# Joined additions, GpSimd Newton steps and a re-ordered start in an attention and MoE kernel

## The chip, the cores and the metric

The kernel runs on one core of one Trainium2 chip. The metric is the device time of one execution in microseconds (us). Five engines matter: TensorE (PE; PEld is its weight load), VectorE (DVE), ScalarE (ACT), GpSimd (POOL) and SyncE (SP), which here issues the DMAs. Each runs its own queue strictly in order and waits on semaphores for the others.

## The reference, cut to what matters

The inputs q, k and v have 2 batches, 8 heads, 768 positions and 64 dimensions. Each head has 16 centroids; every query and key is assigned to the centroid with the largest cosine similarity, and attention is allowed only inside a cluster.

```
q_n, k_n, c_n = each / (norm + 1e-06)
q_assign = argmax(q_n . c_n);  k_assign = argmax(k_n . c_n)
mask   = q_assign[..., :, None] == k_assign[..., None, :]
scores = where(mask, q @ k.T / 8, -1e9)
attn   = exp(scores - max);  attn /= sum(attn) + 1e-9
x = attn @ v                                     # 1536 x 512 after a reshape
h = x @ w_in;  x = (max(h,0) + alpha*min(h,0)) @ w_out
xn = x / rms(x) * rms_g;  x = (silu(xn @ w_gate) * (xn @ w_val)) @ w_out2
```

## The kernel before, in words

**Tiling.** The 16 head-batches are worked off as 8 pairs. A pair has two phases (one half of its 384 query columns each), a phase six slots, one for each tile of 128 keys: slot `6 * ph + t`. In a slot TensorE makes the scores of the tile for both heads (L712 and L713 into one of three rotating `ps_st` banks), ScalarE takes their exponential (`p`, L714), and TensorE multiplies earlier `p` tiles with v (L728). The row maximum of each query has to be known before its exponential, so TensorE also makes the masked scores once ahead (`max_tile`, L662), VectorE reduces them (`mx`, L664; L666 in the first phase), splits the maximum into two parts (`mh`, L671, L672), and TensorE turns them (L690) into rows of the operand `op`.

**What is prepared.** For each pair ahead of its phases: loads (`raw` and `nat`, the transposed and the plain form of q and k), squares (`sq`, ACT L469), sums of squares (`ss`, DVE L483), the reciprocal root (`norm`, `rnorm`), scores against the centroids (`sims`, L516 to L543), the cluster's one-hot code (`arg`: L552 to L565), its transpose (`oht`), and the operand's high part and residual (`hi` L606, `lo` L614, which go to `op` by a DMA). `rnorm` takes two integer operations (L435, L437), three Newton steps and three last operations (L440 to L442). A Newton step is three VectorE operations (L429 to L431), or four GpSimd ones (L423 to L426) for the pairs in `NEWTON`.

**Sums of the softmax.** `pv_tiles` sums `p` over the keys with matmuls against ones (L739, into `ps_sm`). In the phases of `SUMMED` (4 to 12), the first four `p` tiles are added in pairs on VectorE (`pair_add`, L747), so that four operands are left, two sums and two `p`. In the phases of `WHOLE`, here 10 and 11, `pair_join` (L751) adds the two sums in place, and three operands are left.

**Start.** Pairs 0 and 1 have a start of their own (`start`, from L336): squares from `raw`, column sums by a matmul (`ss_rows`, L494), a copy, a turn (`ss_turn`, L503), and `root` (n_y L399, n_e L400, and n_s L403, which copies the sums out of PSUM so that the bank can be used again). `oht_direct(h)` turns the one-hot code of head h of pair 0 by 30 small matmuls for both heads (L589): head 0 into the two-bank tiles `ps_pv` and `ps_mx`, head 1 into `ps_pr` and the three `ps_st` banks; ScalarE copies them to rows 64 to 80 of `op_0` and `op_1` (L598, L600). The first `max_tile` reads `op_0`.

**What sets the order.** Nothing is scheduled at run time. `plan()` puts every step into a slot with an order number inside the slot. The tables `FIRST` to `FIFTH` (pairs 0 to 4) and `PAIR` (pairs 5 to 7) give for each step (slot, order) relative to the pair's first slot, 12 times the pair's number; a negative slot lies in earlier pairs' phases. Steps with one slot are issued by order number, and each engine's queue follows from that. The two MoE layers (L1010 and on) come after the attention.

Of the kernel before, what the change touches and what calls it, by code (L numbers as in the profile page):

```python
# [12 lines left out]
AF = mybir.ActivationFunctionType  # L13
ALU = mybir.AluOpType
# [4 lines left out]
BIG = float(2.0 ** 60)  # L19
# [3 lines left out]
    "load": ((-44, 6.1), (-44, 6.2), (-39, 6.1), (-38, 6.1)),  # L23
    "sq": ((-38, 4), (-36, 1.015)),
    "ss": ((-37, 0.6), (-36, 2.05)),
    "norm": tuple((t, 5 + n / 100) for n, t in enumerate([-32] + [-31] * 6 + [-30] * 7)),
    "hi": ((-28, 1.06), (-27, 1.06)),
    "lo": ((-24, 2.3), (-25, 1.05)),
    "sims": ((-30, 1.6), (-29, 1.7)),
    "scale": ((-29, 1.75),),  # L30
    "arg": ((-27, 5), (-24, 2.1), (-24, 2.2), (-22, 1.62), (-21, 5)),
# [3 lines left out]
FIFTH = {  # L35
    **PAIR,
    "lo": ((-26, 2.3), (-25, 1.05)),
    "load": ((-41, 6.1), (-41, 6.2), (-39, 6.1), (-38, 6.1)),
    "sq": ((-35, 4), (-34, 4)),
    "ss": ((-34, 5), (-33, 5)),  # L40
}
FOURTH = {
    **PAIR,
    "load": ((-38, 6.1), (-38, 6.2), (-30, 6.1), (-30, 6.2)),
    "sq": ((-32, 4), (-32, 4.1)),
    "ss": ((-30, 2.2), (-30, 2.3)),
    "norm": tuple((-27 + n // 6, 5 + (n % 6) / 10) for n in range(17)),
    "hi": ((-27, 4), (-26, 4)),
# [9 lines left out]
    "sq": ((-24, 4), (-23, 4)),  # L58
    "ss": ((-24, 5), (-23, 5)),
    "norm": tuple((-21, 5.1 + n / 100) for n in range(14)) + tuple((-18, 2.41 + n / 100) for n in range(3)),  # L60
    "hi": ((-22, 4), (-21, 4)),
    "lo": ((-18, 2.46), (-14, 6)),
    "sims": ((-20, 1.65), (-18, 1.7)),
    "scale": ((-18, 2.44),),
    "arg": ((-18, 2.45), (-16, 5), (-16, 5.1), (-15, 5), (-14, 5)),
# [23 lines left out]

SUMMED = range(4, 13)  # L90
FULL = (4, 6, 8, 10)
WHOLE = {10: (6, 1.99), 11: (5, 0.59)}
SQUARED = 2
ASIDE = (2,)
NEWTON = (2, 3)
EARLY = (
    (59, 12),
    (70, 2.45),
# [127 lines left out]
class Attention:  # L226
# [52 lines left out]
    def setup(self):  # L279

        nc, C, H, D = self.nc, self.C, self.H, self.D
        v, act, g = nc.vector, nc.scalar, nc.gpsimd
        n, rows = H * C, 2 * C
        cn = self.pre([n, 2, D], "cn")
        css = self.pre([n, 1], "css")
        self.sq0 = self.pre([128, D], "sq0")
        src = self.centroids.rearrange("h c d -> (h c) d")
# [29 lines left out]
        i = self.idf.rearrange("p (e g r) -> p g e r", e=2, r=32)  # L317
# [27 lines left out]
        self.warm(6, self.bk.pv)
        rc = self.bk.st()
        for i in range(0, 128, rows):
            nc.tensor.matmul(rc[i:i + rows, 0:1], lhsT=self.idf[:rows, :rows], rhs=r[:rows], start=True, stop=True)
        act.copy(out=self.rc0, in_=rc[:, 0:1])
        ps = self.bk.pr()  # L350
        self.sims_mm(0, ps)
        self.prep_sq(1, 0)
        simc = self.sims_copy(0, ps, self.rc0)
        ssc = self.ss_rows(0, v.tensor_copy)
        for h in range(2):
            self.prep_dma_a(h)
        for h in range(2):
            self.prep_dma_b(h, 1)
        self.load_v(0)
        steps, rn = self.root(self.ss_turn(ssc), [128, self.T // 2, 4, 2], "n0")  # L360
        self.sims_turn(0, self.bk.st(), simc)
        spread(self.cb, n, act.copy)
        self.prep_sq(1, 1)
        for step in steps:
            step()
        self.norm[0] = None, rn
# [5 lines left out]
        self.sims_mm(1, ps)  # L372
        ssc = self.ss_rows(1, act.copy)
        self.simc[1] = self.sims_copy(1, ps, 1.0)
        self.norm[1] = self.root(self.ss_turn(ssc), [128, self.T // 2, 4, 2], "n1", True)
        act.add_instruction(mybir.InstLoadActFuncSet(name=nc.get_next_instruction_name(), act_func_set_id=EXP_AND_LN,
                                                     ins=[], outs=[]))
        act.activation(out=spare, in_=self.eps[:, 0:1], func=AF.Exp)
        self.warm(4, self.bk.pv)
        self.prep_lo(0, 1)  # L380
        for h in range(2):
            self.oht_direct(h)
        for i in range(2):
            self.prep_hi(1, i)
        v.tensor_tensor_reduce(out=pat, in0=pat, in1=self.idf, scale=1.0, scalar=0.0, op0=ALU.mult, op1=ALU.add,
# [191 lines left out]
    def oht_direct(self, h):  # L577

        nc, X = self.nc, self.T // 2
        if h:  # L580
            hi = [self.bk.pr(), self.bk.st()]
            ps = [[self.bk.st(), self.bk.st()], hi]
        else:
            ps = [b().rearrange("p a b -> p (a b)") for b in (self.bk.mx, self.bk.pv)]
            ps = [[b, b[:, self.HS:]] for b in ps]
        for i in (1, 0):
            for g in range(2):
                for x in range(X):
                    nc.tensor.matmul(ps[i][g][0:16, x * 128:(x + 1) * 128], lhsT=self.oh[0][:, x, h, :, i, g],  # L589
                                     rhs=self.idr, start=True, stop=True)  # L590
        o1 = self.op1[h][64:80]
        for i in (1, 0):
            cuts = ((0, 128), (128, self.S)) if not i else ((0, self.S),)
            parts = [(ps[i][g][:16, :self.HS], o1[:, i, sl]) for g, sl in self.halves()] if h else \
                [(ps[i][0][:16, a:b], o1[:, i, a:b]) for a, b in cuts]
            for src, dst in parts:
                if i:
                    nc.scalar.copy(out=dst, in_=src)  # L598
                else:
                    nc.scalar.activation(out=dst, in_=src, func=AF.Identity, scale=-BIG)  # L600

# [198 lines left out]
    def plan(self):  # L800
# [3 lines left out]
        def at(s, o, fn, *a):  # L804
            ev.setdefault(s, []).append((o, len(ev.get(s, [])), fn, a))
# [4 lines left out]
        for pr in range(self.NP):  # L810
# [564 lines left out]
```

## Time and profile before

| | |
|---|---|
| median of 3 runs | 819.69 us (819.63 to 819.71) |
| profiled execution, device time | 819.63 us |
| its span | 817.9 us |
| PE busy | 809.6 us, 99% |
| DVE busy | 623.7 us, 76% |
| ACT busy | 335.6 us, 41% |
| POOL busy | 362.1 us, 44% |
| granted TensorE clock | 1.00 |

The span is what the profile's times run over; the profiled execution's own time is 1.7 us longer and lies 0.06 us under the median. A busy share of an engine is an average over very different stretches: the first 60 us fill the pipeline, 60 to about 275 us are attention phases, and the rest is matrix multiplication for the MoE layers.

### The profile page before, as it was taken

To read this page: it belongs to the slowest core of one execution; us is meant where nothing else is said; L and a number is where in the kernel's file an instruction comes from. 1 tells how busy PE (TensorE), PEld (TensorE's weight loads), DVE (VectorE), ACT (ScalarE), POOL (GpSimd) and SP (SyncE) were. 2 spreads that over 40 slices of the span, in tenths; PEclk is the share of its full clock that TensorE was granted. 3 is DMA by queue.
4 is the path that set the end of the run, shared out by engine and by line. 5 is a ranking of instruction groups with operands and counts; after the bars stand their busy time and mean duration, and the time that the engine had idled before them with its cause. 6 is when DMAs were issued, how large, how long until landed. Compare 5 with 4: busy or idle time off the path is not lost.

```text
span 817.9 us, 11705 instructions
## 1 busy us (share of the span) xinstructions
PE 809.6 (99%) x4350; PEld 625.0 (76%) x4350; DVE 623.7 (76%) x1036; ACT 335.6 (41%) x652; POOL 362.1 (44%) x335
## 2 busy tenths in 40 slices
PE   8999999999999999999999999999999999999998
PEld 5565666666666888888888888888888888888887
DVE  6989999999998489999999977877555555555523
ACT  7655776666564333433434444432212221222110
POOL 3421221221213267786766772416465546554511
PEclk9999999999999999999999999999999999999999
DMA  8786655754532022232212220102121212121012
GB/s 206 201 229 181 132 154 161 171 111 115 133 114 79 1 77 78 78 103 65 88 59 75 77 78 1 51 1 78 52 77 54 76 52 77 57 73 51 1 52 103
DMA packets 23624, 74.03 MB, mean 91 GB/s; under 512 B 3600, under 2 KB 4752, under 8 KB 23568
## 3 DMA queue, kind: packets, MB, share of 16 engines
q1 hardware_dynamic: 23568, 73.29, 31.3%
q8 instruction: 34, 0.56, 0.3%
q14 instruction: 22, 0.18, 0.1%
HBM read 49.88 MB, written 3.15 MB: 65 GB/s over the span
## 4 chain that ended last, share of the span: by engine, by line
PE 96%; DVE 2%; DMA 1%; ACT 1%; issue 0%; SPq 0%; DVEq 0%; ACTq 0%
PE ps_st L1010 35%; PE ps_mx L1010 14%; PE ps_pv L1010 14%; PE ps_pv L728 8%; PE ps_pr L1010 5%; PE ps_st L712 4%; PE ps_st L713 4%; PE ps_sm L739 3%; PE ps_ma L662 3%; PE ps_mb L662 2%; DMA nat<-in_kn_dram 1%; DVE mx L666 1%; PE ps_pv L393 1%; PE ps_pr L516 1%; PE ps_pr L690 0%; PE ps_pr L782 0%
## 5 line engine op out<-in xcount | busy, mean ns | idle before, releaser
L1077 POOL TENSOR_TENSOR gl<-v,gh 128x512 fp32r<-128x512 f32 x68 | 96.0, 1412 | 143.8 <-ACT gh L1076 142.4
L1076 ACT CAST gh<-v 128x512 fp32r<-128x512 f32 x68 | 42.3, 622 | 151.9 <-DVE v L1073 83.3
L1073 DVE TENSOR_TENSOR v<-ps_st,t 128x512 f32<-128x512 f32 x36 | 24.9, 691 | 100.3 <-PE ps_st L1010 100.2
L714 ACT ACTIVATE p<-ps_st 128x384 f32<-128x384 f32 x192 | 85.3, 491 | 28.1 <-PE ps_st L713 26.6
L992 DVE SCALAR_TENSOR_TENSOR dec_a<-raw,dec_a 128x512 uint32<-128x512 uint32 x66 | 81.6, 1236 | 2.2
L728 PE MATMUL ps_pv<-p,vnat 128*64 128x384 f32 x384 | 72.6, 499 | 0.0
L1069 DVE SCALAR_TENSOR_TENSOR v<-v,alpha,t 128x512 f32<-128x512 f32 x45 | 53.0, 1177 | 21.9 <-ACT v L1068 21.8
L712 PE MATMUL ps_st<-op 128*128 128x384 f32 x192 | 67.8, 353 | 0.3 <-ACT oht L575 0.3
L1010 PE MATMUL ps_st<-x1h,stage 128*128 128x512 f32 x272 | 67.2, 389 | 0.0
L713 PE MATMUL ps_st<-op 82*128 82x384 f32 x192 | 65.0, 339 | 0.0
L1010 PEld LDWEIGHTS ps_st<-x1h,stage 128*128 128x128 f32 x272 | 51.1, 188 | 10.6
L1123 DVE TENSOR_TENSOR x<-ps_mx,x 128x1024 f32<-128x1024 f32 x36 | 43.9, 1220 | 18.7 <-PE ps_mx L1010 18.7
L664 DVE TENSOR_REDUCE mx<-ps_ma 128x1 f32<-128x384 f32 x90 | 49.7, 552 | 10.1 <-PE ps_ma L662 9.2
L798 POOL TENSOR_TENSOR x1l<-X,x1h 128x384 fp32r<-128x384 f32 x15 | 15.9, 1062 | 91.7 <-ACT x1h L795 91.7
L1010 PE MATMUL ps_st<-x1h,wvh 128*128 128x512 f32 x144 | 56.2, 390 | 0.0
L1010 PE MATMUL ps_st<-x1h,wvl 128*128 128x512 f32 x144 | 56.0, 389 | 0.0
L1010 PE MATMUL ps_st<-x1h,wih 128*128 128x512 f32 x132 | 51.6, 391 | 0.0
L1010 PE MATMUL ps_st<-x1h,wil 128*128 128x512 f32 x132 | 51.4, 389 | 0.0
L664 DVE TENSOR_REDUCE mx<-ps_mb 128x1 f32<-128x384 f32 x90 | 49.4, 549 | 0.1
L1123 DVE TENSOR_TENSOR x<-ps_pv,x 128x1024 f32<-128x1024 f32 x35 | 42.5, 1214 | 6.8 <-PE ps_pv L1010 6.8
L990 DVE TENSOR_SCALAR dec_a<-raw 128x512 uint32<-128x512 uint32 x66 | 47.6, 722 | 0.0
L995 DVE SCALAR_TENSOR_TENSOR dec_e<-raw,dec_e 128x512 f32<-128x512 uint32 x66 | 45.7, 692 | 2.3
(304 smaller groups left out, 1998.3 us busy)
## 6 DMA issues: line engine op xcount, KB each, us to landing
raw<-in_moe_w_out_dram SPq DMA_DIRECT2D x28, 512.0 KB, 3.5
op<-stage SPq DMA_DIRECT2D x32, 384.0 KB, 5.9
raw<-in_moe_w_in_dram SPq DMA_DIRECT2D x15, 512.0 KB, 3.6
raw<-in_moe_w_val_dram SPq DMA_DIRECT2D x12, 512.0 KB, 3.4
raw<-in_moe_w_gate_dram SPq DMA_DIRECT2D x12, 512.0 KB, 3.4
op<-stage SPq DMA_DIRECT2D x16, 288.0 KB, 5.9
raw<-in_qt_dram SPq DMA_DIRECT2D x8, 384.0 KB, 4.8
raw<-in_kt_dram SPq DMA_DIRECT2D x8, 384.0 KB, 5.1
```

Source lines behind the costliest of these rows:

```text
L664: nc.vector.tensor_reduce(out=mx[:, g, k:k + 1], in_=to, op=ALU.max, axis=AX.X)
L712: nc.tensor.matmul(ps, lhsT=o1[:, 1, ks], rhs=o1[:, 0, qs], start=True, stop=False)
L713: nc.tensor.matmul(ps, lhsT=o2[:, 1, ks], rhs=o2[:, 0, qs], start=False, stop=True)
L714: nc.scalar.activation(out=self.P[s][:, e], in_=ps, func=AF.Exp, scale=self.scale)
L728: nc.tensor.matmul(ps[64 * e:64 * e + 64], lhsT=self.vnat[ph // 2][:, e, t0 + y], rhs=P[y][:, e], start=t0 + y == 0, stop=t0 + y == T - 1)
L990: lambda: v.tensor_scalar(out=a, in0=top, scalar1=3, scalar2=0x3FFFFFFF, op0=ALU.logical_shift_left, op1=ALU.bitwise_and),
L992: lambda: v.scalar_tensor_tensor(out=a, in0=top, scalar=0xC0000000, in1=a, op0=ALU.bitwise_and, op1=ALU.bitwise_or),
L995: lambda: v.scalar_tensor_tensor(out=ef, in0=bot, scalar=2.0 ** -52, in1=ef, op0=ALU.mult, op1=ALU.mult),
L1010: self.nc.tensor.matmul(ps, lhsT=a, rhs=b, start=first and i == 0, stop=last and i == len(terms) - 1)
L1069: nc.vector.scalar_tensor_tensor(out=v, in0=v, scalar=self.nalpha[:, a], in1=t, op0=ALU.mult, op1=ALU.add)
L1077: nc.gpsimd.tensor_tensor(out=lo, in0=v, in1=f(hi), op=ALU.subtract)
L1123: nc.vector.tensor_tensor(out=dst, in0=ps, in1=dst, op=ALU.add)
```

## The change

Four things are edited.

1. `WHOLE` gets the phases 4 to 9 as well: `pair_join` at the phase's slot 5 order 5 (even phases) or slot 6 order 1.99 (odd phases), so that TensorE sums three operands there instead of four.
2. `NEWTON` gets pairs 5, 6 and 7: their Newton steps go to GpSimd. The table `PAIR` starts the two integer operations earlier (`norm`).
3. The residual of q (`lo`) is moved: for pairs 5 to 7 from slot -24 to slot -19, for pair 2 from -18 to -12. Loads of pair 4, squares of pair 3 and one high part of pair 2 move by some slots.
4. The start is re-ordered. The square of pair 0's k is split between ScalarE and VectorE, the centroids are scaled on ScalarE, both residuals of pair 0 come early, the sums' rows come ahead of the centroids' scores, and both squares of pair 1 follow the copies of the centroids' block. `oht_direct` comes ahead of `root` of pair 1 and of the loading of the activation table, and its copies for head 0 are divided between ScalarE and VectorE.

```
-    "norm": tuple((t, 5 + n / 100) for n, t in enumerate([-32] + [-31] * 6 + [-30] * 7)),
+    "norm": tuple((t, 5 + n / 100) for n, t in enumerate([-34] * 2 + [-33] * 6 + [-32] * 6 + [-30] * 3)),
-    "lo": ((-24, 2.3), (-25, 1.05)),
+    "lo": ((-19, 4.9), (-25, 1.05)),
...
-    "lo": ((-18, 2.46), (-14, 6)),
+    "lo": ((-12, 2.02), (-14, 6)),
...
-WHOLE = {10: (6, 1.99), 11: (5, 0.59)}
+WHOLE = {**{ph: ((5, 5), (6, 1.99))[ph % 2] for ph in range(4, 10)}, 10: (6, 1.99), 11: (5, 0.59)}
-NEWTON = (2, 3)
+NEWTON = (2, 3, 5, 6, 7)
...
+        self.prep_sq(0, 0)
+        self.prep_hi(0, 0)
+        sq, raw = self.nat[0][:, 1].rearrange("p t h d -> p (t h d)"), self.raw[0][:, 1]
+        (_, s0), (_, s1) = self.halves()
+        act.activation(out=sq[:, s0], in_=raw[:, s0], func=AF.Square)
+        v.tensor_tensor(out=sq[:, s1], in0=raw[:, s1], in1=raw[:, s1], op=ALU.mult)
+        self.prep_hi(0, 1)
         for i in range(2):
-            self.prep_sq(0, i)
-        self.prep_hi(0, 0)
-        self.prep_lo(0, 0)
+            act.activation(out=cn[:, i, :], in_=cn[:, i, :], func=AF.Identity, scale=r)
         for i in range(2):
-            v.tensor_scalar(out=cn[:, i, :], in0=cn[:, i, :], scalar1=r, scalar2=None, op0=ALU.mult)
-        self.prep_hi(0, 1)
+            self.prep_lo(0, i)
         self.warm(6, self.bk.pv)
+        ssc = self.ss_rows(0, act.copy)
...
-        self.prep_sq(1, 0)
-        simc = self.sims_copy(0, ps, self.rc0)
-        ssc = self.ss_rows(0, v.tensor_copy)
...
-        self.sims_turn(0, self.bk.st(), simc)
+        self.sims_turn(0, self.bk.st(), self.sims_copy(0, ps, self.rc0))
         spread(self.cb, n, act.copy)
-        self.prep_sq(1, 1)
+        for i in range(2):
+            self.prep_sq(1, i)
...
-        self.norm[1] = self.root(self.ss_turn(ssc), [128, self.T // 2, 4, 2], "n1", True)
+        ss = self.ss_turn(ssc)
+        self.warm(4, self.bk.pv)
+        self.oht_direct(0)
+        self.norm[1] = self.root(ss, [128, self.T // 2, 4, 2], "n1", True)
+        self.oht_direct(1)
         act.add_instruction(mybir.InstLoadActFuncSet(...))
         act.activation(out=spare, in_=self.eps[:, 0:1], func=AF.Exp)
-        self.warm(4, self.bk.pv)
-        self.prep_lo(0, 1)
-        for h in range(2):
-            self.oht_direct(h)
...
+        cuts = (0, 128), (128, self.S)
         for i in (1, 0):
-            cuts = ((0, 128), (128, self.S)) if not i else ((0, self.S),)
-            parts = [(ps[i][g][:16, :self.HS], o1[:, i, sl]) for g, sl in self.halves()] if h else \
+            parts = [(ps[i][g][:16, :self.HS], o1[:, i, sl]) for g, sl in self.halves()] if h or i else \
                 [(ps[i][0][:16, a:b], o1[:, i, a:b]) for a, b in cuts]
-            for src, dst in parts:
+            for n, (src, dst) in enumerate(parts):
+                aside = n == (1 if i else 0) and (i or not h)
                 if i:
-                    nc.scalar.copy(out=dst, in_=src)
+                    (nc.vector.tensor_copy if aside else nc.scalar.copy)(out=dst, in_=src)
+                elif aside:
+                    nc.vector.tensor_scalar(out=dst, in0=src, scalar1=-BIG, scalar2=None, op0=ALU.mult)
                 else:
                     nc.scalar.activation(out=dst, in_=src, func=AF.Identity, scale=-BIG)
```

Lines of the changed kernel are a few higher: L598 and L600 become L604 and L608, L747 and L751 become L755 and L759, L614 becomes L622.

On ScalarE at the end of the start, before: the second square of pair 1, the copy of its sums, the root's n_y, n_e, n_s, the table load, and then the copies to `op_0` and `op_1`.

```order
L469 ACTIVATE nat_240<-raw_149 128x768 [waits DMAHW4_49]
L496 COPY ssc<-ps_st 128x384 [waits DVE_49,PE_49]
L521 ACTIVATE simc<-ps_st 128x384
L399 ACTIVATE n_y<-ps_st,eps 128x24 [waits PE_49]
L400 ACTIVATE n_e<-n_y,eps 128x24 [waits Activation_49]
L403 COPY n_s<-ps_st 128x24
L376 ACT_TABLE_LOAD
L378 ACTIVATE spare<-eps 128x1
L598 CAST op_0_115<-ps_pv 16x768 [waits PE_49]
L600 ACTIVATE op_0_115<-ps_mx 16x128 [waits PE_49]
L600 ACTIVATE op_0_115<-ps_mx 16x640
L598 CAST op_1_116<-ps_pr 16x384 [waits PE_49]
```

The same place on ScalarE after the change.

```order
L474 ACTIVATE nat_276<-raw_149 128x768 [waits DMAHW3_49]
L474 ACTIVATE nat_276<-raw_149 128x768 [waits DMAHW4_49]
L501 COPY ssc<-ps_st 128x384 [waits PE_49]
L526 ACTIVATE simc<-ps_st 128x384 [waits Activation_49]
L604 CAST op_0_115<-ps_pv 16x384 [waits PE_49]
L608 ACTIVATE op_0_115<-ps_mx 16x640 [waits DVE_49]
L404 ACTIVATE n_y<-ps_st,eps 128x24
L405 ACTIVATE n_e<-n_y,eps 128x24 [waits Activation_49]
L408 COPY n_s<-ps_st 128x24
L604 CAST op_1_116<-ps_pr 16x384 [waits PE_49]
L608 ACTIVATE op_1_116<-ps_st 16x384 [waits PE_49] x2
L385 ACT_TABLE_LOAD
```

The root's three operations now stand behind the copies to `op_0`, and the second of these waits for VectorE. VectorE's part there, after the change: the first copy waits for ScalarE.

```order
L570 TENSOR_TENSOR oh<-code,am_289 128x3x16x2 x3
L604 CAST op_0_115<-ps_pv 16x384 [waits Activation_49]
L606 TENSOR_SCALAR op_0_115<-ps_mx 16x128 [waits PE_49]
L604 CAST op_1_116<-ps_st 16x384 [waits PE_49]
L390 ISA pat,ohs<-pat,idf 128x128 [waits Pool_49]
```

On TensorE, after the change, what stands between the turned codes of head 1 and the first `max_tile` (L670). Before, the rows are the same, but the first `max_tile` waits for ScalarE where it now waits for VectorE.

```order
L594 MATMUL ps_pr<-idr,oh 16x128 [waits DVE_49]
L594 MATMUL ps_pr<-idr,oh 16x128 x2
L594 MATMUL ps_st<-idr,oh 16x128 x3
L594 MATMUL ps_st<-idr,oh 16x128 [waits DVE_49,Activation_49]
L594 MATMUL ps_st<-idr,oh 16x128 x2
L594 MATMUL ps_st<-idr,oh 16x128 [waits Activation_49]
L594 MATMUL ps_st<-idr,oh 16x128 x2
L670 MATMUL ps_pv<-op_0_115 128x384 [waits DMAHW5_49,DVE_49]
```

The third `ps_st` bank of this list is the one that `ss_turn` of pair 1 has filled and `root` reads, so the last group waits for n_s in both kernels, and n_s has another place in ScalarE's queue.

On VectorE in phase 5, before: the two sums of squares of pair 6 (`ss`, from its squares `nat`), the argmax's comparison (`sims`) and the residual of pair 5's q.

```order
L664 TENSOR_REDUCE mx<-ps_mb 128x1 [waits PE_49]
L483 TENSOR_REDUCE ss_1649<-nat_1450 128x3x4 [waits Activation_49]
L555 TENSOR_TENSOR sims<-sims,am_1611 128x384 [waits DVE_49]
L557 TENSOR_TENSOR sims<-sims,code 128x384 [waits DVE_49]
L614 TENSOR_TENSOR stage_106<-raw_1237,stage_106 128x768 [waits DMAHW6_49,DMAHW4_49,DMAHW3_49]
L664 TENSOR_REDUCE mx<-ps_ma 128x1 [waits PE_49]
```

The same place after the change.

```order
L672 TENSOR_REDUCE mx<-ps_mb 128x1 [waits PE_49]
L759 TENSOR_TENSOR add_1588<-add_1588,add_1641 128x768 [waits DVE_49]
L488 TENSOR_REDUCE ss_1651<-nat_1465 128x3x4 [waits Activation_49]
L560 TENSOR_TENSOR sims<-sims,am_1613 128x384
L562 TENSOR_TENSOR sims<-sims,code 128x384 [waits DVE_49]
L672 TENSOR_REDUCE mx<-ps_ma 128x1 [waits PE_49]
```

The join stands ahead of the second sum of squares, and the residual is gone from here (it stands at the end of phase 6, ahead of the join there).

On GpSimd, after the change, phase 4: Newton steps of pair 5 between the second split of the output (L783) and the residual of the output tile (L806). Before, these two follow each other.

```order
L783 TENSOR_TENSOR hl<-rs,hl 128x192 [waits Pool_49]
L428 TENSOR_TENSOR n_a<-n_y,ss_1282 128x24 [waits DVE_49]
L429 TENSOR_TENSOR n_a<-n_a,n_y 128x24 [waits Pool_49]
L430 TENSOR_SCALAR n_a<-n_a 128x24 [waits Pool_49]
L431 TENSOR_TENSOR n_y<-n_y,n_a 128x24 [waits Pool_49]
```

The pattern of four is there three times, and again in phases 6 and 8.

## Rows read from the trace of the kernel before

**Rows 1.** The page: busy times and the chain that ended last, by engine.

```profile
PE 809.6 (99%) x4350; PEld 625.0 (76%) x4350; DVE 623.7 (76%) x1036; ACT 335.6 (41%) x652; POOL 362.1 (44%) x335
...
PE 96%; DVE 2%; DMA 1%; ACT 1%; issue 0%; SPq 0%; DVEq 0%; ACTq 0%
```

**Rows 2.** Windows, all engines: stretch, length, busy us, clock, DMA share, GB/s.

```profile
20.00:30.00 10.00, 9.27 (x60) 5.77 (x59) 9.34 (x21) 5.95 (x11) 3.73 (x8) 1.00 1.01 263
30.00:40.00 10.00, 9.65 (x71) 5.71 (x71) 9.69 (x26) 7.75 (x15) 6.14 (x17) 1.00 0.45 140
```

**Rows 3.** Timeline of the start: start, duration, engine, line [idle before].

```profile
7.72 0.56 ACT L521 ACTIVATE simc<-ps_pr,rc 128x384 f32<-128x384 f32 x1
...
9.14 0.28 ACT L399 ACTIVATE n_y<-ps_st,eps 128x24 f32<-128x24 f32 x1 [0.87 <-PE ps_st L503]
...
10.11 0.84 ACT L469 ACTIVATE nat<-raw 128x768 f32<-128x768 f32 x1
...
13.01 0.28 ACT L399 ACTIVATE n_y<-ps_st,eps 128x24 f32<-128x24 f32 x1 [0.24 <-PE ps_st L503]
...
13.54 0.16 ACT L403 COPY n_s<-ps_st 128x24 f32<-128x24 f32 x1
13.71 1.28 ACT L376 ACT_TABLE_LOAD   x1
...
14.21 0.52 PE L589 MATMUL ps_pv<-idr,oh 128*16 128x128 f32 x6 [0.31 <-DVE oh L565]
...
15.93 0.84 ACT L600 ACTIVATE op<-ps_mx 16x128 fp32r<-16x128 f32 x2
...
16.24 0.62 PE L662 MATMUL ps_pv<-op 80*128 80x384 f32 x2 [0.44 <-ACT op L600]
16.68 0.45 ACT L598 CAST op<-ps_pr 16x384 fp32r<-16x384 f32 x1
```

**Rows 4.** Timeline, the residual of pair 2's q on VectorE.

```profile
40.97 0.95 DVE L614 TENSOR_TENSOR stage<-raw,stage 128x768 fp32r<-128x768 f32 x1
```

**Rows 5.** Chain of waits: start, length, sums of one phase.

```profile
104.70 1.44 PE ps_sm L739 x32
...
188.15 1.11 PE ps_sm L739 x24
```

**Rows 6.** Timeline of phase 5, VectorE, GpSimd and TensorE.

```profile
116.65 1.83 POOL L614 TENSOR_TENSOR stage<-raw,stage 128x768 fp32r<-128x768 f32 x1
...
117.60 0.94 DVE L483 TENSOR_REDUCE ss<-nat 128x12 f32<-128x768 f32 x1
...
118.89 0.83 PE L739 MATMUL ps_sm<-p,ones 128*32 128x192 f32 x16
...
123.76 0.17 DVE L672 SCALAR_TENSOR_TENSOR mh<-mx,mh 128x6 fp32r<-128x6 f32 x1
...
123.99 0.40 PE L690 MATMUL ps_pr<-idr,mh 128*64 128x128 f32 x3
```

**Rows 7.** Timeline, VectorE and GpSimd at work together.

```profile
118.46 0.55 DVE L555 TENSOR_TENSOR sims<-sims,am 128x384 f32<-128x384 f32 x1
...
172.34 1.82 POOL L614 TENSOR_TENSOR stage<-raw,stage 128x768 fp32r<-128x768 f32 x1
...
173.70 0.87 DVE L555 TENSOR_TENSOR sims<-sims,am 128x384 f32<-128x384 f32 x1
```

**Rows 8.** Timeline of phase 4, a maximum and a Newton operation on VectorE.

```profile
100.90 0.56 DVE L664 TENSOR_REDUCE mx<-ps_ma 128x1 f32<-128x384 f32 x1
...
101.51 0.44 PE L662 MATMUL ps_ma<-op 80*128 80x384 f32 x1
...
102.04 0.18 DVE L429 TENSOR_TENSOR n_a<-n_y,ss 128x24 f32<-128x24 f32 x1
```

**Rows 9.** Timeline, a Newton operation of pair 2 on GpSimd, twice.

```profile
36.71 0.83 POOL L423 TENSOR_TENSOR n_a<-n_y,ss 128x24 f32<-128x24 f32 x1
...
38.23 0.23 POOL L426 TENSOR_TENSOR n_y<-n_y,n_a 128x24 f32<-128x24 f32 x1
```

More of the change, by code (lines that the diff above doesn't have):

```diff
@@ L37 @@
     "lo": ((-26, 2.3), (-25, 1.05)),
-    "load": ((-41, 6.1), (-41, 6.2), (-39, 6.1), (-38, 6.1)),
+    "norm": tuple((t, 5 + n / 100) for n, t in enumerate([-32] + [-31] * 6 + [-30] * 7)),
+    "load": ((-41, 6.1), (-41, 6.2), (-35, 2.7), (-35, 2.8)),
     "sq": ((-35, 4), (-34, 4)),
@@ L44 @@
     "load": ((-38, 6.1), (-38, 6.2), (-30, 6.1), (-30, 6.2)),
-    "sq": ((-32, 4), (-32, 4.1)),
+    "sq": ((-33, 4), (-32, 4)),
     "ss": ((-30, 2.2), (-30, 2.3)),
@@ L60 @@
     "norm": tuple((-21, 5.1 + n / 100) for n in range(14)) + tuple((-18, 2.41 + n / 100) for n in range(3)),
-    "hi": ((-22, 4), (-21, 4)),
-    "lo": ((-18, 2.46), (-14, 6)),
+    "hi": ((-22, 4), (-22, 4.1)),
+    "lo": ((-12, 2.02), (-14, 6)),
     "sims": ((-20, 1.65), (-18, 1.7)),
@@ L358, in setup @@
             self.prep_dma_b(h, 1)
+        self.prep_dma_b(0, 2)
         self.load_v(0)
         steps, rn = self.root(self.ss_turn(ssc), [128, self.T // 2, 4, 2], "n0")
-        self.sims_turn(0, self.bk.st(), simc)
+        self.sims_turn(0, self.bk.st(), self.sims_copy(0, ps, self.rc0))
         spread(self.cb, n, act.copy)
-        self.prep_sq(1, 1)
+        for i in range(2):
+            self.prep_sq(1, i)
         for step in steps:
@@ L821, in plan @@
             if pr == 0:
-                at(-12, -1, self.prep_dma_b, 0, 2)
                 at(-12, 1, self.prep_dma_b, 1, 2)
```

## The prediction

> **What bounds the kernel now.** I read the page first. TensorE is busy 99% of the span and has 96% of the chain that ended last [rows 1]. So a change counts if it takes work from TensorE, or gives or takes a wait there. The windows come next. From 20 to 40 us TensorE has gaps, and VectorE is busy 9.34 and 9.69 of each 10 us [rows 2], so VectorE paces that stretch: what starts it late ends it late. The clock column is 1.00 throughout. After about 60 us TensorE is full, but VectorE is not far behind, and whether an edit there costs is a matter of margins at single instructions. I took these from the timeline.
>
> The base of the sum is the profiled execution's own time, 819.63 us, 0.06 under the median of the runs. The span and what lies around it (1.7 us) enter only through it.
>
> **Part 1, the start.** The first `max_tile` begins at 16.24 [rows 3]. I follow its new chain.
>
> The second square of pair 1 ended at 10.95 (10.11 and 0.84). Before, ScalarE did the first square (also 0.84) and the copy of the scores (0.56) ahead of n_y of pair 0 and then stood idle 0.87. Now both stand behind n_y: +1.4. n_y comes earlier by at most that idle 0.87; I take 0.6, as the square of k is halved over two engines. ScalarE's copies of the centroid block now wait for TensorE's turn of the late scores; I take 0.3 for that. So the second square is later by 1.4 - 0.6 + 0.3 = 1.1 (estimate; 0.8 to 1.5), and the sums, their turn and the warming matmuls behind it with it. TensorE reached the turned codes (L589) 0.31 before 14.21, at 13.90; now it reaches them at 15.0. The one-hot code is not later than that, so it no longer decides.
>
> From there, before, it was 2.03 to the first maximum, with the table load (1.28) in ScalarE's way. Now six matmuls 0.52; ScalarE copies half of `op_0` in 0.45, the row of that shape at 16.68; VectorE's half comes only after it, at the same 0.45; VectorE's 16x128 piece some 0.2; ScalarE's 16x640, which waits for that, 0.6 of the 0.84 of both pieces. With 0.05 to 0.1 at each change of engine that ends at 17.35. Then the root: n_y to the end of n_s took 13.01 to 13.70, 0.69. It ends at 18.05. The last group of L589, which stands ahead of the first maximum in TensorE's queue, needs the bank that n_s frees, and adds 0.2. The first maximum then begins at about 18.3, later by 2.0. The bounds are +0.4 (if the squares' delay is hidden and n_s is not last, only the chained copies) and +2.2. The table load leaves this path and lands where ScalarE has time.
>
> The Trainium skill ("PSUM — Partial Sum Buffer", section "PSUM bank collisions raise a hardware error") says that two engines may not touch one bank and partition quarter at once, reads included, so that a dependency is put between them. By that page the copies of one bank run in turn, as I have them; the rows of the kernel before hold no such shared copy.
>
> What is given back: VectorE is idle for 0.97 of 20 to 40 us [rows 2], and part of it waits for transfers that have their own time; I take 0.2 (0 to 0.97). The residual that stood at 40.97 for 0.95 [rows 4], in a stretch that VectorE still paces, moves by six slots to a place where VectorE waits anyway; I take 0.5 (0 to 0.87, its length less overlap). Start: 2.0 - 0.2 - 0.5 = **+1.3** (-0.3 to +2.0).
>
> **Part 2, the sums.** A phase with four operands takes 1.44 in the chain, one with three 1.11 [rows 5]. Six phases change: 6 x 0.33 = **-2.0**.
>
> **Part 3, the joins in phases 5 and 7.** The join takes 0.95, as the residual of the same shape and two inputs does [rows 4]; the residual of q leaves this stretch, so VectorE's work is even. But the join comes at 117.60 in place of the sum of squares [rows 6], and GpSimd runs its own residual from 116.65 to 118.48. The rows that tell what happens then: L555, with two inputs from SBUF, takes 0.55 when GpSimd is done (118.46), and 0.87 when it starts at 173.70 inside GpSimd's L614, which ends at 174.16 [rows 7]. It ended 0.41 after that, so all but 0.14 of it waited. The join would end at 118.48 + 0.95 - 0.14 = 119.29 and not at 118.55: 0.74 late. TensorE's last sums begin at 118.89, so they wait 0.4. Further on, VectorE's delay stays until mh (123.76 to 123.93), for which TensorE's L690 (123.99) has a margin of 0.06. So TensorE is late by about 0.73 there and the 0.33 of this phase is lost: against part 2 +1.06. Phase 7 repeats the pattern. Two phases: **+2.1** (0.5 to 2.3). The lower end is no lock at all: VectorE's balance is even, mh stays put, and most of the 0.33 goes into that wait, some 0.23 in each. Phase 9 has the residual of 172.34 to 174.16 too, but its last sums start later after it; there I cost nothing.
>
> The Trainium skill ("SBUF — State Buffer", section "Who interferes with whom") states this as a rule: a VectorE instruction with two SBUF inputs and a GpSimd one that reads SBUF exclude each other for the whole length of whichever came first, while a reduction takes no part. The 0.87 agrees with it.
>
> **Part 4, Newton steps in phases 4, 6 and 8.** On VectorE nine operations at 0.18 go [rows 8], about 1.9 with the gaps, and the join (0.87 net) comes, in phases 6 and 8 the residual (0.87) too. The work is again even or less. On GpSimd twelve come at 0.23, or up to 0.83 beside VectorE [rows 9]; GpSimd does nothing else between two of its pieces there, and the next use of the result is late enough. What can cost: the two integer operations (0.18 each) stand about 0.4 earlier in VectorE's queue, and VectorE's additions now meet GpSimd's reads. The maximum that frees a bank for TensorE ends at 101.46 and TensorE takes the bank at 101.51 [rows 8]: 0.05 of margin. A delay of 0.4 there gives a stall of 0 to 0.5; I take 0.3, in three phases **+0.9** (-0.3 to 1.5; below nothing if the freed VectorE time takes away a short wait).
>
> The Trainium skill ("Perfetto Trace Analysis", section "Optimizing Scalar/DVE Operations") says that moving work between these two may not help, since they share a read port. By it the moved steps would give nothing; by the rows, 0.83 for 0.23, too.
>
> **Sum.** 1.3 - 2.0 + 2.1 + 0.9 = +2.3, to 819.63: 821.9, and with the 0.06 to the median **822.0 us**. Other moves (loads of pair 4, squares of pair 3, the high part of pair 2) I cost at nothing: their results are needed some slots later; if the cover were gone for the squares, ScalarE would wait for a load of pair 3, and the range's room above the forecast holds that.
>
> **Rivals.**
> - *The joins and Newton steps are free* (no exclusion of the two engines as I price it). The place is the join of phase 5; it decides whether it ends before 118.89. For it: VectorE's work there is even. Against it: the 0.87. Then four phases gain 0.33 and the two odd ones 0.1, because of mh: -1.5, and with the start's +1.3: -0.2, **819.5**, not slower.
> - *The start is free*: the first maximum at most 0.4 late, that is n_s is not what it waits for, or ScalarE gets through sooner, and 0.7 is given back: -0.3. With parts 2 to 4 (+1.0): **820.4**. Against it: the queue shows the wait.
> - *Both are free*: -0.3 - 1.5: **817.9**, faster.
> - *The clock drops*: TensorE idles about 2 us ahead of the first maximum, where before it had 0.44. At the lower of the two levels, 1.2 against 2.4 GHz, its work of the next 1 to 2 us takes double, +1.0: **823.0**. Against it: the clock was 1.00 through the gaps before.
>
> **How the numbers follow.** My forecast has 0.45, and its own range is 821.0 to 823.4. The joins free: 0.17; the start free: 0.15; both: 0.13; the clock: 0.10. About 0.2%, 1.64 us, is what a measurement of this kernel tells from no change, so slower begins at 821.3 and faster below 818.05. Slower: 0.42 of the forecast's 0.45 (the rest lies at its lower edge) and the clock's 0.10: 0.52. Faster: 0.13, and 0.05 from the first rival's lower side: 0.18. The rest, 0.30, is the same. The range of 8 in 10 leaves out the upper tail beyond 823.6 and the lower half of the both-free case: 818.0 to 823.6.
>
> **What would show it.** In the profile after: the first maximum (L670) at 18.0 to 18.5 with TensorE waiting for n_s ahead of it; a shift of about 1.3 left at 60 us; L739 in pieces of 1.11 in phases 4 to 9; the join of phase 5 (relative to its surroundings) about 1.7 long, ending 0.8 after GpSimd's residual, and TensorE's L690 late behind mh; in phases 4, 6 and 8 short TensorE waits for mx. The forecast is wrong if the first maximum is under 17 us, if the joins take 0.95, or if waits that I have not seen (a transfer for pairs 2 to 4, ScalarE behind the moved high part) open up beyond 0.5 us.

## The result and the profile after

The changed kernel takes 826.16 us (median of 6 runs, 825.66 to 826.93) against 819.83 beside it (819.63 to 821.0): a ratio of 1.0077, 95% interval 1.0064 to 1.0090. It is slower by 6.3 us, where 2.3 were forecast and the range ended at 823.6. The direction and the mechanisms of parts 2 and 3 were right; the start cost three times what I had for it, and phase 10 cost 0.72 where I had nothing.

The profiled execution has a span of 823.9 against 817.9. The chain that ended last, by engine, answers to the second line of [rows 1]: VectorE's share went from 2 to 5%.

```profile
PE 94%; DVE 5%; ACT 0%; issue 0%; DVEq 0%
```

TensorE's own waits, of the changed kernel (line and tile, what it waited for, us in total, times, longest). The first, the third and the fourth are new.

```profile
PE ps_st L594 <- ACT n_s L408: 1.9, 1, 1.9
PE ps_pv L398 <- DVE zero L1283: 1.4, 1, 1.4
PE ps_st L532 <- ACT simc L526: 1.2, 1, 1.2
PE ps_sm L747 <- DVE add L759: 1.0, 3, 0.5
PE ps_ma L670 <- DVE mx L672: 0.8, 3, 0.3
```

To place the 6.0 us by which the spans differ I subtracted the start of the same TensorE instruction in both profiles: the turned codes (L589; by the rows 24 small matmuls and not 30), the first `max_tile` (L662), and the turns of the maxima (L690), of which there is one in each phase. The numbers of the table are such differences, in us after the kernel before; the heads of the last columns are the times in the kernel before and the phases in which they lie (ph 4 is at 111, ph 11 at 206). The other kernels are those of the experiments.

```
kernel            codes  first max   61    111   124   139   152   167   180   193   206
                                          ph 4   5     6     7     8     9    10    11
changed            1.86     3.34    4.21  4.19  4.93  4.91  5.67  5.64  5.32  6.04  6.03
old start          0.55     0.57    0.73  0.70  1.45  1.42  2.17  2.16  1.83  2.56  2.55
start alone        1.34     2.93    4.91  4.94  4.94  4.96  4.96  4.98  4.98  4.98  4.97
root first         1.24     1.14    0.89  0.87  1.62  1.59  2.36  2.34  2.01  2.72  2.72
filled wait        1.23     2.72    2.42  2.40  3.15  3.13  3.90  3.87  3.55  4.27  4.26
start mended       0.14     0.10   -0.16 -0.18  0.56  0.52  1.28  1.25  0.93  1.65  1.63
sum before join    1.86     3.34    4.18  4.16  4.31  4.18  4.34  4.20  3.88  4.59  4.57
no odd joins       1.88     3.38    4.27  4.26  4.14  4.00  3.91  3.78  3.46  4.17  4.17
residual 7 back    1.81     3.31    5.26  5.26  6.01  5.98  6.74  6.72  6.95  7.07  7.07
integers back      1.38     2.87    4.75  5.06  5.83  6.91  7.69  8.78  8.48  9.21  9.20
mended st. alone  -0.13    -0.17   -0.16 -0.16 -0.16 -0.15 -0.13 -0.11 -0.11 -0.11 -0.12
all mended         0.38     0.35    0.10  0.09 -0.03 -0.17 -0.30 -0.44 -0.77 -0.77 -0.71
```

Read the first row. The start makes 4.21. Phases 4, 6 and 8 add nothing (-0.02 each), phases 5 and 7 add 0.75 each, phase 9 gives back 0.32, phase 10 adds 0.72.

The timeline of the start after the change, against [rows 3] (start, duration, engine, line, [idle before]):

```profile
6.12 1.55 PE L499 MATMUL ps_st<-nat,hs 128*32 128x384 f32 x8
...
9.13 0.28 ACT L404 ACTIVATE n_y<-ps_st,eps 128x24 f32<-128x24 f32 x1 [0.84 <-PE ps_st L508]
...
11.03 0.42 ACT L329 COPY cb<-ps_pr 64x64 f32<-64x64 f32 x2 [0.80 <-PE ps_pr L326]
11.48 1.58 ACT L474 ACTIVATE nat<-raw 128x768 f32<-128x768 f32 x2
...
16.07 0.55 PE L594 MATMUL ps_pv<-idr,oh 128*16 128x128 f32 x6
...
16.65 0.47 ACT L604 CAST op<-ps_pv 16x384 fp32r<-16x384 f32 x1 [1.78 <-PE ps_pv L594]
...
17.15 0.55 DVE L604 CAST op<-ps_pv 16x384 fp32r<-16x384 f32 x1 [2.49 <-ACT op L604]
...
17.93 0.69 ACT L608 ACTIVATE op<-ps_mx 16x640 fp32r<-16x640 f32 x1 [0.81 <-DVE op L606]
...
18.63 0.28 ACT L404 ACTIVATE n_y<-ps_st,eps 128x24 f32<-128x24 f32 x1
...
19.38 0.37 PE L594 MATMUL ps_st<-idr,oh 128*16 128x128 f32 x3 [1.86 <-ACT n_s L408]
...
19.58 0.57 PE L670 MATMUL ps_pv<-op 80*128 80x384 f32 x2
```

The squares of pair 1 end at 13.06 instead of 10.95, the codes are turned at 16.07, and then the chain runs as foreseen: ScalarE, VectorE, ScalarE, root, n_s. What it leads to is in the windows (stretch, length, busy us of PE, PEld, DVE, ACT, POOL, then the granted clock, DMA share, GB/s):

```profile
18.00:19.00 1.00, 0.00 (x0) 0.00 (x0) 0.66 (x3) 0.96 (x3) 0.00 (x0) 1.00 0.98 249
...
22.00:23.00 1.00, 1.00 (x4) 0.81 (x4) 0.76 (x2) 1.00 (x3) 0.00 (x0) 0.50 0.96 356
...
24.00:25.00 1.00, 1.00 (x8) 0.87 (x6) 0.70 (x1) 0.00 (x0) 0.00 (x0) 0.71 1.04 406
25.00:26.00 1.00, 1.00 (x8) 0.91 (x7) 0.96 (x1) 0.47 (x1) 0.00 (x0) 1.00 1.06 366
```

TensorE stands still for 1.9 us, and some 2 us after it has begun again the granted clock is 0.50, the lower level, for a little over 3 us.

Phase 5 after the change, against [rows 6]: GpSimd's residual, the join, the sums that wait for it, the turn of the maxima.

```profile
120.84 1.82 POOL L622 TENSOR_TENSOR stage<-raw,stage 128x768 fp32r<-128x768 f32 x1
...
121.80 1.69 DVE L759 TENSOR_TENSOR add<-add,add 128x768 f32<-128x768 f32 x1
...
123.54 0.53 PE L747 MATMUL ps_sm<-add,ones 128*32 128x192 f32 x8 [0.28 <-DVE add L759]
...
128.92 0.39 PE L698 MATMUL ps_pr<-idr,mh 128*64 128x128 f32 x3
```

The join takes 1.69 and ends 0.83 after GpSimd's residual. In phase 4 it takes 0.94. GpSimd stands idle there for 1.93, up to 107.82:

```profile
106.35 0.94 DVE L759 TENSOR_TENSOR add<-add,add 128x768 f32<-128x768 f32 x1
...
107.82 1.00 POOL L806 TENSOR_TENSOR x1l<-X,x1h 128x384 fp32r<-128x384 f32 x1 [1.93 <-ACT x1h L803]
```

Phase 10 is the place that I had not priced: pair 7's residual of q now stands there, the join comes after it and meets GpSimd's `x1l`.

```profile
191.40 0.95 DVE L622 TENSOR_TENSOR stage<-raw,stage 128x768 fp32r<-128x768 f32 x1
...
192.91 1.00 POOL L806 TENSOR_TENSOR x1l<-X,x1h 128x384 fp32r<-128x384 f32 x1 [7.78 <-ACT x1h L803]
...
193.19 1.53 DVE L759 TENSOR_TENSOR add<-add,add 128x768 f32<-128x768 f32 x1
...
194.77 0.53 PE L747 MATMUL ps_sm<-add,ones 128*32 128x192 f32 x8 [0.51 <-DVE add L759]
```

In phase 4 TensorE's lateness grows from 4.23 to 4.51 before the shorter sums give 0.32 back. The listed waits for `mx` (0.8, three times) are not these: they lie at 59.01, where the kernel before waits too, and in phases 5 and 7. In phase 4 there are two holds (0.10 and 0.07), in which the tile begins 0.06 after the end of the maximum that frees its bank, and the first of the two tiles takes 0.44 instead of 0.34:

```profile
103.62 0.54 DVE L672 TENSOR_REDUCE mx<-ps_mb 128x1 f32<-128x384 f32 x1
...
104.22 0.44 PE L670 MATMUL ps_mb<-op 80*128 80x384 f32 x1
...
105.42 0.54 DVE L672 TENSOR_REDUCE mx<-ps_ma 128x1 f32<-128x384 f32 x1
...
106.02 0.45 PE L670 MATMUL ps_ma<-op 80*128 80x384 f32 x1
```

### The profile page after: what moved, and what is told of

Its sections match the earlier page's. It is cut to its first block, busy times and chain, and to the rows that moved or that the text cites. A ratio compares the mean times of both kernels' runs of the same rounds, so it can differ in the third digit from the quotient of the medians.

```text
span 823.9 us, 11623 instructions
## 1 busy us (share of the span) xinstructions
PE 812.3 (99%) x4302; PEld 624.6 (76%) x4302; DVE 628.0 (76%) x1016; ACT 335.3 (41%) x653; POOL 375.3 (46%) x371
## 4 chain that ended last, share of the span: by engine, by line
PE 94%; DVE 5%; ACT 0%; issue 0%; DVEq 0%
PE ps_st L1017 34%; PE ps_mx L1017 14%; PE ps_pv L1017 14%; PE ps_pv L736 7%; PE ps_pr L1017 5%; PE ps_st L720 4%; PE ps_st L721 3%; PE ps_ma L670 3%; PE ps_sm L747 3%; PE ps_mb L670 2%; DVE mx L672 2%; PE ps_pv L398 1%; PE ps_pr L521 1%; DVE add L759 1%; PE ps_pr L698 0%
## 5 line engine op out<-in xcount | busy, mean ns | idle before, releaser
L806 POOL TENSOR_TENSOR x1l<-X,x1h 128x384 fp32r<-128x384 f32 x15 | 15.9, 1060 | 74.0 <-ACT x1h L803 74.0
L1004 POOL TENSOR_TENSOR dec_a<-dec_a,woh 128x512 f32<-128x512 f32 x24 | 37.6, 1566 | 21.7 <-DVE dec_e L1001 16.1
```

## Experiments

**Old start.** The start of the kernel before, all else as changed (the start's code of the diff taken back).

> The changed kernel with the start of the kernel before (its order of squares, copies, root and turned codes); the tables, joins and Newton steps stay as changed. Theory: start and phases are separate sums. In the changed kernel TensorE is 4.2 us late at 60 us and gains only 1.8 more by 210 us, so here about 819.8 + 1.8 = 821.6 (821.2 to 822.0). Rival: the late start worsens the phases too (the loads of later pairs collide differently), then under 820.8. Rival: the phases would have cost more but the late start gave them slack, then over 822.5.

Measured: 822.87, ratio 1.0030 (1.0018 to 1.0043). From 111 to 206 it loses 1.85, as the changed kernel does (1.84): start and phases add up. The total lies over the range and over the line that I had set for the last rival (822.5), but the table does not bear that rival out: the phases cost what they cost in the changed kernel. The old start of the profiled execution was itself late by 0.57. The first row below says why: here its matmuls at 6.33 took 1.45, in the kernel before 0.89 for the same eight; the second row is n_y behind them. The median lies another 0.65 over the profiled execution: four of the six have a mean granted clock of 0.998 and take 822.74 to 823.17, the two at 1.000 take 821.59 and 822.22.

```profile
6.33 1.45 PE L517 MATMUL ps_pr<-raw,cb 128*32 128x384 f32 x8
...
9.70 0.28 ACT L400 ACTIVATE n_y<-ps_st,eps 128x24 f32<-128x24 f32 x1 [1.20 <-PE ps_st L504]
```

**Start alone.** The kernel before with the changed start.

> The kernel before with the changed start alone. Theory: first maximum at 19.6, clock at its lower level for some 3 us after it, TensorE 4.2 to 4.4 us late at 60 us, nothing later: 819.8 + 4.3 = 824.1 (823.6 to 824.6). Rival (the start's loss is partly due to the moved residual of pair 2): under 823.4.

Measured: 824.67, ratio 1.0058 (1.0045 to 1.0070). The table has 4.9 at 61 and nothing later; the lower clock lasted from 19 to past 25 here, and the lateness grew by 2.0 from the first maximum to 36 us instead of 1.1. The total lies 0.07 over the range.

**Root first.** The two lines of the root of pair 1 change places with head 0's codes:

```
-        ss = self.ss_turn(ssc)
+        self.norm[1] = self.root(self.ss_turn(ssc), [...], "n1", True)
         self.warm(4, self.bk.pv)
         self.oht_direct(0)
-        self.norm[1] = self.root(ss, [...], "n1", True)
```

> The changed kernel with the root of pair 1 put back ahead of the turned codes of head 0 on ScalarE. Theory: TensorE's wait of 1.9 for n_s goes, the chained copies (ScalarE, VectorE, VectorE, ScalarE) remain, first maximum at 18.7 instead of 19.6. If the clock still falls behind a shorter wait: 826.2 - 0.9 = 825.3. If it stays at 1.00: 824.3 or less. Rival (n_s is not what the first maximum waits for, the copies alone set it): no change, 826.2.

Measured: 822.87, ratio 1.0035 (1.0023 to 1.0048), 3.3 under the changed kernel. The wait for n_s and the fall of the clock went together. But the first maximum came 1.3 earlier than I expected:

```profile
17.01 0.27 DVE L605 TENSOR_SCALAR op<-ps_mx 16x128 fp32r<-16x128 f32 x1
...
17.32 0.69 ACT L607 ACTIVATE op<-ps_mx 16x640 fp32r<-16x640 f32 x1 [0.81 <-DVE op L605]
17.35 0.30 PEld L669 LDWEIGHTS ps_pv<-op 80*128 80x128 f32 x2 [0.45 <-issue]
17.38 0.59 PE L669 MATMUL ps_pv<-op 80*128 80x384 f32 x2 [0.30 <-issue]
```

Of this, 0.7 is a misreading of mine: the first maximum needs only VectorE's 16x128 piece, not ScalarE's 16x640. In the changed kernel nothing but n_s, queued behind both, held it. The other 0.62 is no effect of the edit: the eight matmuls at 6.12 took 0.94 in this execution and 1.55 in the changed kernel's, so its codes were turned 0.62 earlier. In the two profiles the 3.3 is 0.62 of this, 1.58 from the codes to the first maximum (3.51 to 1.93) and 1.12 after it, where the clock stayed at 1.00.

**Filled wait.** Five matmuls against zeros ahead of the group that waits for n_s:

```
             for g in range(2):
+                if h and g > i:
+                    self.warm(5, self.bk.pv)
```

> The changed kernel with five matmuls against zeros, into a bank that is free from 17.7 on, ahead of the group that waits for n_s: TensorE's wait of 1.9 there is mostly filled with work that nobody needs. Theory (the wait lowers the granted clock, and that lower clock is what made the start late by another 1.1 to 2.2 after the first maximum): first maximum at the same 19.6 or a little later, clock 1.00 from 20 to 27 us, 826.2 - 1.1 to - 2.1 = 824.1 to 825.1. Rival (the lateness that grows after the first maximum is VectorE's or the transfers'): 826.2 or later.

Measured: 824.44, ratio 1.0050 (1.0038 to 1.0063), 1.7 under the changed kernel. The wait is filled, n_s still ends as long after the codes as it did, and from codes to first maximum it takes 3.52 as in the changed kernel (3.51). The codes were turned 0.63 earlier, since the eight matmuls at the start took 0.95 in this execution; that part of the gain is not the edit's. After it nothing grows: 2.72 becomes 2.42 by 61 us, where the changed kernel went from 3.34 to 4.21. The window and two rows:

```profile
20.00:26.00 6.00, 5.06 (x29) 3.76 (x29) 5.76 (x12) 4.24 (x7) 0.00 (x0) 1.00 0.99 308
```

```profile
17.13 1.43 PE L398 MATMUL ps_pv<-zero 128*128 128x512 f32 x5 [0.24 <-DVE op L606]
18.75 0.37 PE L596 MATMUL ps_st<-idr,oh 128*16 128x128 f32 x3 [0.20 <-ACT n_s L408]
```

So TensorE's standing still was paid twice, as a wait and as a lower clock; filling it saved the second payment, some 1.2. The other executions agree. Their mean granted clock is 1.000 in four of five here (0.998 in the fifth), and 0.998 or less in 32 of 33 of the six kernels that wait 1.9 for n_s. But the wait is not the only thing that a lower clock comes with: in the kernels without it, the kernel before among them, 18 of 98 executions have 0.998 or less too, and no profile was taken of one of these.

**Start mended.** The changed kernel with its start put right: first square of pair 1 and copy of the scores ahead of the root of pair 0, root of pair 1 first, head 0's tiles copied whole, one by each engine.

```
+        self.prep_sq(1, 0)                     # ahead of ss_rows(0)
...
+        simc = self.sims_copy(0, ps, self.rc0) # ahead of root "n0"
...
-                [(ps[i][0][:16, a:b], o1[:, i, a:b]) for a, b in cuts]
+                [(ps[i][0][:16, :self.S], o1[:, i, :self.S])]
```

> The changed kernel with four things put right in the start: the first square of pair 1 and the copy of the scores ahead of the root of pair 0 on ScalarE, the root of pair 1 ahead of the turned codes, and head 0's two tiles copied whole, one by ScalarE and one by VectorE, so that no copy waits for the other engine. Theory: turned codes at 14.3 (14.9 if the first column sums run at the slower rate), first maximum at 15.8 to 16.4 against 16.24 before, no fall of the clock; the phases' 1.8 remain: 820.9 (820.4 to 821.7). Rival (the fall of the clock or the transfers, not ScalarE's order, make the start late): over 823.

Measured: 821.61, ratio 1.0009 (1.0000 to 1.0019), 4.6 under the changed kernel. Codes at +0.14, first maximum at +0.10, and -0.16 at 61. The start's loss lies in the steps put right here. Their shares are not all separated, but the whole copies gave nothing on this path: from codes to first maximum it takes 1.99 here and 1.93 in "root first", where they are still divided. The split square of k, the centroids on ScalarE and an earlier transfer for pair 0 (`prep_dma_b(0, 2)`, which the list of the change does not name) are kept here and cost nothing that shows.

**Sum before join.** One number: the second sum of squares ahead of the join in phases 5 and 7.

```
-    "ss": ((-37, 0.6), (-36, 2.05)),
+    "ss": ((-37, 0.6), (-36, 1.98)),
```

> The changed kernel with the second sum of squares (a reduction) ahead of the join in phases 5 and 7, one line of a table. Theory of the exclusion of VectorE's two-input operation and GpSimd's residual: the reduction runs during GpSimd's 1.83, the join starts as that ends and takes 0.95; TensorE still waits some 0.6 for it but mh is no longer late; TensorE's lateness at L698 of phases 5 and 7 falls from +0.75 to about +0.3 each, 826.2 - 0.9 = 825.3. Rival (the join takes 1.69 because of its own size or place, not because of GpSimd): it would take 1.69 here as well, and the time rises.

Measured: 824.88, ratio 1.0058 (1.0046 to 1.0071), 1.3 under the changed kernel. GpSimd's residual runs from 120.82 to 122.64 here. The reduction beside it is not slowed, and the same join takes 0.95:

```profile
120.82 1.82 POOL L622 TENSOR_TENSOR stage<-raw,stage 128x768 fp32r<-128x768 f32 x1
...
121.77 0.94 DVE L488 TENSOR_REDUCE ss<-nat 128x12 f32<-128x768 f32 x1
122.62 0.95 DVE L759 TENSOR_TENSOR add<-add,add 128x768 f32<-128x768 f32 x1
```

Phases 5 and 7 cost 0.15 instead of 0.75. The exclusion is shown; the rival, a join that is long by itself, falls. The gain was larger than expected, since phases 6 and 8 gave back another 0.13 each.

**No odd joins.** `WHOLE` without 5 and 7.

> The changed kernel without the joins of phases 5 and 7. Theory (the collision with GpSimd's residual makes these two phases late by 0.75 each at L698): that lateness goes, four operands come back there but VectorE has 0.87 less to do; net per phase about 0 instead of +0.75, so 826.2 - 1.5 = 824.7. Rival (their lateness comes from the Newton steps or the moved residual): 826.2 or above.

Measured: 824.47, ratio 1.0045 (1.0030 to 1.0060), 1.7 under. Phase 4 now gives 0.01 and each of the phases 5 to 8 gives 0.09 to 0.14: TensorE has its four operands back in two of them and is still faster.

**Residual of pair 7 back.**

```
             tab = (FIRST, ...)[min(pr, 5)]
+            if pr == 7:
+                tab = {**PAIR, "lo": ((-24, 2.3), (-25, 1.05))}
```

> The changed kernel with the residual of q of pair 7 at its old place (slot -24, order 2.3); those of pairs 5 and 6 stay moved. Theory: in phase 10 this residual now stands ahead of a join that the kernel before had too, the join comes 0.87 later, meets GpSimd's x1l and takes 1.53, and TensorE is 0.72 late; without it phase 10 costs 0: 826.2 - 0.7 = 825.5. Back in phase 9 the residual stands behind the join there, where VectorE has idle time. Rival (phase 10 is late because phase 9's gain of 0.33 is spent at a fixed point, or because of the Newton steps): 826.2.

Measured: 826.23, ratio 1.0063 (1.0047 to 1.0079): no gain, which is the time that the rival had. The start of this execution is 1.05 later at 61 us, with the lower clock for close to 7 us, so only the phases can be compared: from 61 to 206 it loses 1.81, the changed kernel 1.82. The table shows why: phase 10 falls from 0.72 to 0.12, but phase 9 rises from -0.32 to +0.23. There the residual follows a join that GpSimd's residual has already lengthened:

```profile
180.43 1.28 DVE L759 TENSOR_TENSOR add<-add,add 128x768 f32<-128x768 f32 x1
...
182.69 0.95 DVE L622 TENSOR_TENSOR stage<-raw,stage 128x768 fp32r<-128x768 f32 x1
```

Phases 9 and 10 together cost 0.40 in one and 0.35 in the other. So it was not the residual's place alone: phase 9 has taken a join, and the residual costs beside it as it does in phase 10. A fixed point that takes phase 9's gain, as the rival has it, is not there: "all mended" keeps that gain through phase 10.

**Integers back.** Pairs 5 to 7: integer operations behind the second addition, last operations ahead of the scale.

```
+    "norm": ((-32, 5),) + tuple((-31, 5 + n / 100) for n in range(1, 14)) + ((-29, 1.72), (-29, 1.73), (-29, 1.74)),
```

> The changed kernel with the two integer operations of pairs 5 to 7 at their old place on VectorE (behind the second addition), the Newton steps behind them on GpSimd, the three last operations just ahead of the scale. Theory: in phases 4, 6 and 8 the gain of 0.33 from the sums is lost in short waits of TensorE for the maxima because VectorE stands 0.4 later; with the operations back these waits go: 826.2 - 0.9 = 825.3 if all of it, 825.9 if the join alone makes a third wait. Rival (the even phases' gain is lost by VectorE's additions waiting for GpSimd's Newton operations): no change or slower.

Measured: 828.86, ratio 1.0102 (1.0084 to 1.0119): 2.7 slower than the changed kernel, where a gain was expected. That is the time that the rival had, but the rows show the theory at work and a new loss behind it. In phase 4 the lateness is 4.77 up to the sums and 4.45 behind them: the holds for the maxima are gone and the 0.32 of the sums is there. In phase 6 it is likewise 5.83 and 5.52.

```profile
103.80 0.55 DVE L672 TENSOR_REDUCE mx<-ps_mb 128x1 f32<-128x384 f32 x1
...
104.66 0.34 PE L670 MATMUL ps_mb<-op 80*128 80x384 f32 x1
```

The loss comes after that. The Newton steps now start late, so that `x1l` on GpSimd falls beside VectorE's L777, and the three last operations have left VectorE's idle time for a busy place:

```profile
141.50 1.01 POOL L806 TENSOR_TENSOR x1l<-X,x1h 128x384 fp32r<-128x384 f32 x1
...
141.61 1.12 DVE L777 SCALAR_TENSOR_TENSOR rs<-rs,ys 128x192 f32<-128x192 f32 x1
142.66 0.17 DVE L445 TENSOR_TENSOR n_y<-n_y,ss 128x24 f32<-128x24 f32 x1
```

L777 (L769 in the kernel before) took 0.36 there; in phase 6 TensorE then waits 0.60 for the next maximum and 0.26 for mh.

**Mended start alone**, in the kernel before.

> The kernel before with the mended start alone. Theory: the start's loss was the order on ScalarE and the clock, not the transfers or the split of the squares: first maximum at 16.3 as before, nothing later: the same as the kernel before within 0.3. Rival (the give-back of 0.25 near 40 us needs the moved residual of pair 2): then 0.1 to 0.3 over the kernel before instead of under it.

Measured: 820.03 against 820.12, ratio 0.9995 (0.9986 to 1.0004): the same. The first maximum is at 16.07, and nothing is given back after it: -0.17 there and -0.16 at 61.

**All mended.** The mended start, `WHOLE` without 5 and 7, and pair 7's residual behind the join of phase 10 (slot -18, order 2.3).

> The mended start, joins in phases 4, 6, 8 and 9 but not in 5 and 7, and pair 7's residual of q right behind the join of phase 10, where VectorE has 1.5 us idle. Theory, by sums of what the runs showed: start -0.15, phases 4 to 8 -0.45, phase 9 -0.32, phase 10 0: 0.9 under the kernel before, 818.9 to 819.4 beside 819.8 to 820.3. If the residual in its third place still makes phase 10 late: 0.2 under it or the same.

Measured: 818.93 against 820.12, ratio 0.9983 (0.9974 to 0.9992): as forecast, and faster than both kernels, by 0.17% than the kernel before. Phase 10 costs 0.00. The residual there meets `x1l` and takes 1.77, but in time in which VectorE has nothing else to do:

```profile
187.32 1.77 DVE L620 TENSOR_TENSOR stage<-raw,stage 128x768 fp32r<-128x768 f32 x1
189.01 0.55 DVE L670 TENSOR_REDUCE mx<-ps_ma 128x1 f32<-128x384 f32 x1
```

## Why the prediction was wrong, and where it was right

**Part 1, the start: the term that failed.** +1.3 was forecast, +4.2 measured, in four pieces: the codes 1.86 late, 1.48 more up to the first maximum, 1.13 more behind it, 0.27 given back.

- The second square. I had it 1.1 late; it was 2.1. The step "n_y comes earlier ... I take 0.6" did not come true: n_y stood at 9.13 as before (9.14). TensorE's eight matmuls of the column sums took 1.55, and where they took 0.94 (root first) n_y was 0.6 earlier, as forecast. Like against like the step holds: with the old start and slow first matmuls n_y stood at 9.70. So 0.6 of the 4.2 is the difference between two executions and not the edit, and that the kernel before was profiled in a fast one was chance. The other 0.4 is mostly the wait of ScalarE's copies for TensorE's turn of the late scores: 0.80, where I had 0.3.
- From codes to first maximum: 3.3 forecast, 3.5 measured. Right, and n_s was what held it, as the queue had shown.
- The clock: a rival with 0.10 in the forecast, at +1.0, and not a term of the sum. It fell in every profiled kernel that waits 1.9 for n_s and in no other profiled one, for 3 to 7 us, and cost 1.1 to 2.2. "The clock was 1.00 through the gaps before" was no evidence: those gaps were at most 0.7 behind the first matmul, this one 1.9.
- The give-back: 0.7 forecast, 0.27 measured (4.47 to 4.20 between 36 and 48, likewise 0.25 in the mended start). It is missing where the tables are the old ones ("start alone", 4.9 late, and "mended start alone") and also where only the start is ("old start", 0.57 to 0.73). So the idle time of VectorE in 20 to 40 us gave nothing, and the moved steps of pairs 2 to 4, the residual among them, about half of what I took for the residual, and that only together with the new start; no run shows why.

The bounds of the start's term (-0.3 to +2.0) were also narrower than its own pieces allow: with all of the largest give-backs the first is -1.4, with none the second is +2.2.

**Part 2, the sums, and part 3, the joins of 5 and 7: right.** Each phase's sums are 0.33 shorter (1.44 to 1.11). The join was to end 0.81 after GpSimd's residual and ended 0.83 after it; L690 was to be 0.73 late and was 0.75 (the working as it stands, 0.74 less a margin of 0.06, gives 0.68). Against the Trainium skill's rule ("SBUF — State Buffer", section "Who interferes with whom"), the rows here agree: the two-input join waits, but for some 0.12, to the end of GpSimd's instruction, the reduction of 0.94 does not.

**Part 4, the Newton steps: right** (+0.3 against each -0.33, measured -0.02 per phase). In phase 4 the maxima on VectorE end 0.39 later against TensorE than before: 0.29 by the two integer operations ahead of them, 0.08 by the codes' operations (L570, 0.84 instead of 0.76) beside GpSimd's Newton steps. "Integers back" takes both away, and the holds are gone in phases 4 and 6. The two shares are read from lengths; no run separates them.

**Left out: phase 10, +0.72.** "Phase 9 ... there I cost nothing" was right for phase 9 (-0.32 against the -0.33 forecast). But the residual that left phase 9 went to phase 10, ahead of a join that the kernel had before, and I priced the place that it left and not the one that it came to. The two experiments make it a matter of both phases: with the added join of phase 9, phases 9 and 10 together cost 0.35 to 0.40 whether the residual stands behind the join of phase 9 or ahead of that of phase 10, and give 0.33 where it stands behind the latter ("all mended").

The phases 4 to 9 sum to +1.11 against +1.04 forecast; phase 10 adds 0.72, and the start 2.9 over its term.

## What to carry to other kernels

When an instruction is moved back in one engine's queue, look up who waits for its semaphore on another engine, and price that wait twice: its length, and the granted clock of TensorE behind it. When a step is moved out of a stretch, read the stretch that it goes to as closely as the one that it leaves. A VectorE instruction with two inputs from SBUF should not start beside a long GpSimd instruction, where a reduction can: changing the order of the two was worth 1.3 us here. Before two profiles are subtracted, compare the first matmuls and the clock of both executions.

## What the runs showed of the hardware that was not expected

TensorE's first real matmuls do not run at one rate in all executions. Eight of 128x384 that start at 6.12 took 1.55 in the changed kernel (0.85 each) and 0.94 where the root is first (0.50 each), with the same instructions ahead of them and a clock column of 1.00 in both. That moves the whole start by 0.6 us. The Trainium skill ("TensorE: Matmul & The Clock Gate", section "What's actually happening") says that the array starts at the lower of its two levels and that the point at which it rises varies from one execution to the next. The 0.85 and the 0.50 would fit that, but the column in the profile does not show it, so the cause stays open.

The fall of the clock behind the wait of 1.9 us differs too. It comes some 2 us after TensorE has begun again in the changed kernel and lasts a little over 3 us; in "start alone" it comes as TensorE begins again and lasts close to 7 us. The changed kernel's six runs spread over 1.3 us.
